# Attention values as weights in four column tiles, with the exponentials moving

## The chip, the cores and the metric

The kernel runs on one core of a Trainium2 chip. The metric is the device time in microseconds (us) of one execution. Before the change it is 306.41 us, the median of 3 runs (304.89 to 308.06). The engines are TensorE (PE, with its weight loads shown apart as PEld), VectorE (DVE), ScalarE (ACT), GpSimd (POOL) and SyncE (SP), which issues the DMAs.

## The reference

One sequence of 2048 tokens with 512 features is normalised and sent through two branches, whose results are added to the input.

```python
xn = layernorm(x)
# branch A: sliding-window attention, H = 32 heads of Dh = 16, window W = 256
q, k, v = split(xn @ wqkv)
scores = einsum('bhqd,bhkd->bhqk', q, k) * Dh ** -0.5
mask = (i - j >= 0) & (i - j < W)
p = softmax(where(mask, scores, -1e9))
A = einsum('bhqk,bhkd->bhqd', p, v) @ wo
# branch B: gated MLP with a mix over tokens
z = gelu(xn @ w_in)                       # 2048 x 1376
z1, z2 = z[:, :688], layernorm(z[:, 688:])
g = w_sp @ z2 + b_sp                      # 2048 x 2048 times 2048 x 688
B = (z1 * g) @ w_out
out = x + A + B
```

## The kernel before, in words

The tokens are cut into 16 blocks of 128. The program has two stages.

The first stage (up to about 61 us) normalises the blocks, transposes them into `xnT`, computes all of `z` (`do_z`, L419) with the GELU on ScalarE, normalises `z2`, and computes the first projections (the list `early`: keys and queries of the first four blocks, and the values of `VRING - 1` blocks). The reciprocal standard deviations come from a power on GpSimd (`rpow`, L254). GpSimd's queue begins with constants, a memset of the ones in `v_ring` (L378) and of the padding of `u_sb` (L380).

The second stage runs eight kinds of units in an order that the class `Plan` works out before the program is built. `Plan` holds estimated times for the units and lists them one after the other. Each engine then executes its own instructions strictly in that order. The units are:

- `quad`: scores of one key block against up to three query blocks for four heads, as four matmuls of 32 rows side by side in the array (L587), into two PSUM tiles of `ps_s` (three buffers). ScalarE then takes the exponential of each tile into `E` (L595). `E` has keys on the partitions and queries along the row. A head pair shares 32 rows: `k_ring` exists twice, with odd and with even heads set to zero (`emask`).
- `mask`: GpSimd (L604) cuts the diagonal block and VectorE (L609) the far block.
- `unit_av`: the value product of one query block and half of the heads (16). For each head and each of up to three key blocks, a 128x128 block of `E` is loaded as weights and 17 columns of `v_ring` move: 16 values and a column of ones, whose product is the row sum (L624). The result `o_t` has queries on the partitions. VectorE takes the reciprocal of the 16 row sums (L636) and multiplies (L637) into `o_norm`. After the second half, a DMA transpose on SP's queue (L645) makes `oT`, with features on the partitions.
- `unit_q`, `unit_k`, `unit_v`: further projections (L294, L271, L309), copied out of PSUM by VectorE (L304, L284, L318) into rings.
- `unit_g`: one of 16 matmuls of the mix over tokens (L513). After the last, VectorE forms the gated product `u_sb` (L520), and a DMA transposes it into `uT` (L527).
- `unit_out`: part 0 multiplies `oT` with `wo` (L552), part 1 adds `uT` with `w_out` (L558). VectorE adds the residual `x_ch` (L562), and SP stores the block (L563) and loads the next residual.

Three facts set the order of the work around the change. `unit_av`, the projections and `unit_out` all write into the pool `ps_y`, which has a single buffer: the next of them can start on TensorE only when VectorE has read the last one. `unit_g` has a bank of its own (`ps_g`), and its matmuls, with the score matmuls, are placed between the users of `ps_y`. And `E` has `EBUFS` buffers, which a value product frees; a `quad` that needs one waits for it. The last three outputs come after the planned order, in `ps_s`.

Of the kernel before, what the change touches and what calls it, by code (L numbers as in the profile page):

```python
# [8 lines left out]
P = 128  # L9
BF = mybir.dt.bfloat16  # L10
F32 = mybir.dt.float32
ACT = mybir.ActivationFunctionType
ALU = mybir.AluOpType

S_TOK = 2048
D = 512
H = 32
DH = 16
# [4 lines left out]
NDC = D // P  # L23
# [4 lines left out]
NFC = UPAD // P  # L28
Z_RANGES = [(0, 512), (512, FH)]
QRING = 8  # L30
VRING = 5
EBUFS = 12
X_DMA = 8


# [4 lines left out]
class Plan:  # L40


    PROJ = 0.86
    AV_PAIR = 0.0255
    OUT_MM = 0.215
    GCH = 0.144
    LAT = 0.36
# [13 lines left out]
    def run(self, proj, n_out_inline):  # L61
# [8 lines left out]
        o_at, u_at = {}, {}  # L70
# [3 lines left out]
        pend = []  # L74
# [4 lines left out]
        while qi < len(quads) or ai < len(avs) or oi < len(outs) or gi < len(gs) or proj:  # L79
            for rec in list(pend):  # L80
                if rec[0] <= self.tp + 0.2:
                    pend.remove(rec)
                    kb, G = rec[1]
# [7 lines left out]
            cand = []  # L91
            tq = 1e9
            if qi < len(quads):
                kb, G, e = quads[qi]
                ok = True
                if e == 0:
                    i = 4 * kb + G - EBUFS
                    if i >= 0:
                        k2, g2 = divmod(i, 4)
# [8 lines left out]
                if ok:  # L108
                    a, b = (2 * qi) % 3, (2 * qi + 1) % 3
# [3 lines left out]
            if ai < len(avs):  # L113
                qb, h = avs[ai]
                keys = [(kb, G) for kb in range(max(0, qb - 2), qb + 1) for G in (2 * h, 2 * h + 1)]
                if all(k in masked for k in keys) and not any(
# [3 lines left out]
                    n = sum(1 for k in keys) * 8  # L120
# [8 lines left out]
            if oi < len(outs):  # L129
                n, part = outs[oi]  # L130
# [5 lines left out]
            if gi < len(gs):  # L136
                n, hf, c = gs[gi]
                cand.append((self.gfree if c == 0 else 0.0, 5, "g", self.GCH))
            now = [x for x in cand if x[0] <= self.tp + 0.05]
            if not now:  # L140
                m = min(x[0] for x in cand)
# [9 lines left out]
            if pick[2] == "quad":  # L151
                kb, G, e = quads[qi]
                w = nblk(kb)
                order.append(("quad", kb, G, e))
                a, b = (2 * qi) % 3, (2 * qi + 1) % 3
                dur = {3: 0.755, 2: 0.55, 1: 0.34}[w]
                lat = self.LAT - 0.05 * (3 - w)
                for s in (a, b):
                    self.ta = max(self.ta, self.tp + lat) + dur
                    self.sfree[s] = self.ta + self.BACK  # L160
                self.tp += 0.14 + 0.054 * w
                if e == 1:
                    pend.append((self.ta + 0.05, (kb, G)))
                qi += 1
            elif pick[2] == "av":
                qb, h = avs[ai]
                order.append(("av", qb, h))
                self.tp += pick[3]
                self.yfree = self.evac(0.72)
                if h == 1:  # L170
                    o_at[qb] = self.yfree + 2.3
                av_emitted.add((qb, h))
                ai += 1
            elif pick[2] == "proj":
                p = pick[4]
                proj.remove(p)
                order.append(("proj", p[2], p[3]))
                self.tp += pick[3]
                self.yfree = self.evac({"k": 1.2, "q": 0.7, "v": 0.7}[p[2]])
                done_proj[(p[2],) + p[3]] = self.yfree  # L180
            elif pick[2] == "out":
                n, part = outs[oi]
                order.append(("out", n, part))
                self.tp += pick[3]
                if part == 1:
                    self.yfree = self.evac(0.7)
                oi += 1
            else:
                n, hf, c = gs[gi]
                order.append(("g", n, hf, c))  # L190
                self.tp += self.GCH
                if c == NB - 1:
                    self.gfree = self.evac(0.52)
                    if hf == 1:
                        u_at[n] = self.gfree + 2.3
                gi += 1
# [6 lines left out]
def kernel(  # L203
# [12 lines left out]
    nc = tc.nc  # L216
# [11 lines left out]
    z2_all = pers.tile([P, NB, FH], BF, name="z2_all")  # L228
    q_ring = pers.tile([P, NG, QRING * P], BF, name="q_ring")
    k_ring = pers.tile([P, NG, 2, QRING * P], BF, name="k_ring")  # L230
    v_ring = pers.tile([P, VRING, H, DH + 1], BF, name="v_ring")
    fmask = pers.tile([P, P], BF, name="fmask")
    emask = pers.tile([P, 2], F32, name="emask")
    esel = pers.tile([P, 4], F32, name="esel")
    b_bf = pers.tile([P, NB], BF, name="b_bf")
    b_all = pers.tile([P, NB], F32, name="b_all")
    mvx = pers.tile([P, NB, 2], F32, name="mvx")
# [68 lines left out]
    def unit_v(n, on_act=False):  # L306
        m = ps_y.tile([P, 512], F32, name="m", tag="y")
        for c in range(NDC):
            nc.tensor.matmul(  # L309
                m[:], lhsT=xnT[:, c, n * P : (n + 1) * P], rhs=wqkv[:, c, 2 * D : 3 * D],  # L310
                start=(c == 0), stop=(c == NDC - 1),
            )
        dst = v_ring[:, n % VRING, :, 0:DH]
        src = m[:].rearrange("p (h d) -> p h d", d=DH)
        if on_act:
            nc.scalar.copy(out=dst, in_=src)
        else:
            nc.vector.tensor_copy(out=dst, in_=src)  # L318
# [4 lines left out]
    with tc.tile_pool(name="win_pool", bufs=1) as winp, tc.tile_pool(  # L323
# [51 lines left out]
            out=esel[:], in_=esel[:], pattern=[[32, 4]], compare_op=ALU.is_ge,  # L375
            fill=0.0, base=DH - 1, channel_multiplier=-1,
        )
        nc.gpsimd.memset(v_ring[:, :, :, DH : DH + 1], 1.0)  # L378
        for u_sb in u_sbs:
            nc.gpsimd.memset(u_sb[:, FH:UPAD], 0.0)  # L380

# [66 lines left out]
        for n in range(NB + 3):  # L448
            if n < NB:
                transpose_x(n)  # L450
            if n + 3 < NB:
                norm_apply(n + 3)
            if n in stats_at:
                lo, hi = stats_at[n][0], stats_at[n][-1] + 1
                for i in range(lo, hi):
                    x_stats(i)
                rs_x(lo, hi)
            if n == 2:
                nc.vector.tensor_reduce(
                    out=emask[:, 0:1], in_=esel[:], op=ALU.add, axis=mybir.AxisListType.X  # L460
                )
                nc.vector.tensor_scalar(
                    out=emask[:, 1:2], in0=emask[:, 0:1], scalar1=-1.0, scalar2=1.0,
                    op0=ALU.mult, op1=ALU.add,
                )
                nc.vector.tensor_copy(out=b_all[:], in_=b_bf[:])
            if 2 <= n < NB + 2:
                do_z(n - 2, 1)
            if n >= 6 and early:
                f, a = early.pop(0)  # L470
                f(*a, on_act=True)
            if n >= 3:
                do_z(n - 3, 0)
                z2_stats(n - 3)
                if n % 2 == 0:
                    rs_z(n - 4, n - 2)
                elif n >= 5:
                    z2_norm(n - 5)
                    z2_norm(n - 4)
# [4 lines left out]
            f(*a, on_act=True)  # L484

    ep = ctx.enter_context(tc.tile_pool(name="ep", bufs=EBUFS))
    onp = ctx.enter_context(tc.tile_pool(name="onp", bufs=2))
    otp = ctx.enter_context(tc.tile_pool(name="otp", bufs=3))
    utp = ctx.enter_context(tc.tile_pool(name="utp", bufs=2))
    cpool = ctx.enter_context(tc.tile_pool(name="cpool", bufs=2))  # L490
    wsp_pool = ctx.enter_context(tc.tile_pool(name="wsp_pool", bufs=2))
# [48 lines left out]
    def unit_out(n, part, tail=False):  # L540
        if part == 0:
            load_xres(n)
            if tail:
                t = ps_s.tile([P, 2, 512], F32, name="mt", tag="S")
                fo_tiles[n] = t[:, 0, :]
            else:
                t = ps_y.tile([P, 512], F32, name="fo", tag="y")
                fo_tiles[n] = t[:]
            fo = fo_tiles[n]
            oT = oT_tiles.pop(n)  # L550
            for c in range(NDC):
                nc.tensor.matmul(fo, lhsT=oT[:, c, :], rhs=wo_sb[:, c, :], start=(c == 0), stop=False)  # L552
            return
        fo = fo_tiles.pop(n)
        uT = uT_tiles.pop(n)
# [55 lines left out]
                in1=fmask[:].unsqueeze(1).to_broadcast([P, 8, P]), op=ALU.mult,  # L611
            )

    o_state = {}

    def unit_av(qb, half):
        o_t = ps_y.tile([P, 16, DH + 1], F32, name="o_t", tag="y")
        kbs = [kb for kb in (qb - 2, qb - 1, qb) if kb >= 0]
        for g2 in range(2):
            G = 2 * half + g2  # L620
            for j in range(8):
                h = 8 * G + j
                for i, kb in enumerate(kbs):
                    nc.tensor.matmul(  # L624
                        o_t[:, 8 * g2 + j, :],
                        lhsT=E_tiles[(kb, G)][:, qb - kb, j, :],
                        rhs=v_ring[:, kb % VRING, h, :],
                        start=(i == 0),
                        stop=(i == len(kbs) - 1),
                    )  # L630
            E_tiles.pop((qb - 2, G), None)
        if half == 0:
            o_state["n"] = onp.tile([P, D], BF, name="o_norm")
        o_n = o_state["n"]
        rsum = sml.tile([P, 16], F32, name="rsum")
        nc.vector.reciprocal(out=rsum[:], in_=o_t[:, :, DH])  # L636
        nc.vector.tensor_tensor(  # L637
            out=o_n[:, half * 256 : (half + 1) * 256].rearrange("p (h d) -> p h d", d=DH),
            in0=o_t[:, :, 0:DH],
            in1=rsum[:].unsqueeze(2).to_broadcast([P, 16, DH]),  # L640
            op=ALU.mult,
        )
        if half == 1:
            oT = otp.tile([P, NDC, P], BF, name="oT")
            nc.sync.dma_start_transpose(out=oT[:], in_=o_n[:])  # L645
            oT_tiles[qb] = oT

    load_wsp(0)
    load_wsp(1)
# [60 lines left out]
```

## Time and profile before

| what | value |
|---|---|
| median of 3 runs | 306.41 us |
| profiled execution | 304.67 us |
| its span, from first to last instruction | 302.9 us |
| mean granted TensorE clock | 0.996 |
| last value product (L624) begins its last weight load | 284.7 us |
| value products, matmuls | 1440, of 171 ns each, overlapping |
| reciprocal of row sums (L636) | 32 of 258 ns |
| normalising multiply (L637) | 32 of 425 ns |

Busy time is the sum of an engine's instruction times. Matmuls overlap in a pipeline, so TensorE's busy time is no measure of how near it is to its peak. In a group's line, the figures after the bar are the busy time in us, the mean of one in ns, and the idle time just before them with what ended it. The chain that ended last is followed back from the last instruction, and its shares say which engine the end waited for.

### The profile page before, as it was taken

To read this page: it belongs to the slowest core of one execution; us is meant where nothing else is said; L and a number is where in the kernel's file an instruction comes from. 1 tells how busy PE (TensorE), PEld (TensorE's weight loads), DVE (VectorE), ACT (ScalarE), POOL (GpSimd) and SP (SyncE) were. 2 spreads that over 40 slices of the span, in tenths; PEclk is the share of its full clock that TensorE was granted. 3 is DMA by queue.
4 is the path that set the end of the run, shared out by engine and by line. 5 is a ranking of instruction groups with operands and counts; after the bars stand their busy time and mean duration, and the time that the engine had idled before them with its cause. 6 is when DMAs were issued, how large, how long until landed. Compare 5 with 4: busy or idle time off the path is not lost.

```text
span 302.9 us, 7530 instructions
## 1 busy us (share of the span) xinstructions
PE 281.2 (93%) x3168; PEld 153.8 (51%) x3168; DVE 168.0 (55%) x343; ACT 219.4 (72%) x315; POOL 91.1 (30%) x100
## 2 busy tenths in 40 slices
PE   1799999989998999899999999999998999999991
PEld 0465555534443556365555555555554555565640
DVE  4689995547755436355565654565486465342311
ACT  3378766699998798788788888768866788877100
POOL 6213420123433243222333322232222133444200
PEclk9999999999999999999999999999999999999998
DMA  7991237000416151714242624151514163425421
GB/s 231 306 299 36 46 60 156 0 3 0 103 38 123 38 113 38 108 43 102 66 97 56 87 56 105 44 98 48 112 37 91 41 107 80 95 54 97 63 60 55
DMA packets 68849, 25.67 MB, mean 85 GB/s; under 512 B 59936, under 2 KB 68304, under 8 KB 68816
## 3 DMA queue, kind: packets, MB, share of 16 engines
q1 hardware_dynamic: 68768, 25.19, 37.4%
q8 instruction: 25, 0.41, 0.6%
q14 instruction: 8, 0.07, 0.1%
q0 software_dynamic: 48, 0.00, 0.1%
HBM read 8.41 MB, written 2.10 MB: 35 GB/s over the span
## 4 chain that ended last, share of the span: by engine, by line
PE 83%; DMA 5%; DVE 4%; issue 3%; ACT 2%; SPq 1%; POOL 0%; DVEq 0%; POOLq 0%; ACTq 0%
PE gf L513 26%; PE o_t L624 12%; PE S L587 10%; PE zs L419 10%; PE fo L558 6%; PE m L271 5%; PE m L294 4%; PE fo L552 4%; PE m L309 4%; DMA xs<-in_A_x_dram 2%; DMA x_ch<-in_A_x_dram 2%; DMA uT<-u_sb 1%; DMA oT<-o_norm 1%; DVE E L609 1%; PE tp L408 1%
## 5 line engine op out<-in xcount | busy, mean ns | idle before, releaser
L595 ACT ACTIVATE E<-S 128x768 bf16<-128x768 f32 (+2 forms) x256 | 179.4, 772 | 39.2 <-issue 23.8
L604 POOL TENSOR_SCALAR_AFFINE_SELECT E<-E 128x1024 bf16<-128x1024 bf16 x64 | 73.6, 1150 | 148.6 <-ACT E L595 145.8
L513 PE MATMUL gf<-z_all,wspT 128*128 128x344 bf16 x512 | 92.8, 311 | 0.9 <-DVE u_sb L520 0.7
L513 PEld LDWEIGHTS <-wspT 128*128 128x128 bf16 x512 | 43.3, 97 | 32.9 <-issue 12.8
L609 DVE TENSOR_TENSOR E<-E,fmask 128x1024 bf16<-128x1024 bf16 x56 | 46.2, 825 | 2.3 <-ACT E L595 1.9
L587 PE MATMUL S<-q_ring,k_ring 32*128 32x384 bf16 (+2 forms) x576 | 44.6, 303 | 2.2 <-ACT E L595 2.1
L624 PEld LDWEIGHTS <-E 128*128 128x128 bf16 x1440 | 40.0, 96 | 4.3 <-issue 2.4
L419 PE MATMUL zs<-w_in_sb,xnT 128*128 128x512 bf16 (+1 forms) x256 | 41.8, 317 | 0.0
L624 PE MATMUL o_t<-v_ring,E 128*128 128x17 bf16 x1440 | 41.3, 171 | 0.2 <-DVE q_ring L304 0.2
L427 ACT ACTIVATE z_all<-zs 128x688 bf16<-128x688 f32 x32 | 23.8, 743 | 14.0 <-PE zs L419 14.0
L587 PEld LDWEIGHTS <-k_ring 32*128 32x128 bf16 x576 | 14.2, 91 | 35.9 <-issue 35.1
L419 PEld LDWEIGHTS <-xnT 128*128 128x128 bf16 x256 | 23.1, 100 | 16.5 <-issue 1.3
L636 DVE RECIPROCAL rsum<-o_t 128x16 f32<-128x16 f32 x32 | 8.2, 258 | 35.8 <-PE o_t L624 35.8
L562 DVE TENSOR_TENSOR out_sb<-fo,x_ch 128x512 bf16<-128x512 f32 x13 | 9.0, 692 | 31.0 <-PE fo L558 31.0
L520 DVE SCALAR_TENSOR_TENSOR u_sb<-gf,b_all,z_all 128x344 bf16<-128x344 f32 x32 | 18.3, 572 | 13.6 <-PE gf L513 13.6
L558 PE MATMUL fo<-w_out_sb,uT 128*128 128x512 bf16 x78 | 20.4, 382 | 0.8 <-DMA uT<-u_sb 0.8
L284 DVE TENSOR_TENSOR k_ring<-m,emask 128x1024 bf16<-128x1024 f32 x12 | 14.7, 1223 | 8.4 <-PE m L271 8.4
L259 DVE BATCH_NORM_STATS2 st<-z_all 128x6 f32<-128x344 bf16 x32 | 14.9, 506 | 6.3 <-ACT z_all L427 6.3
L309 PE MATMUL m<-wqkv,xnT 128*128 128x512 bf16 x64 | 16.5, 380 | 1.0 <-DVE k_ring L284 0.9
L294 PE MATMUL m<-xnT,wqkv 128*128 128x512 bf16 x64 | 16.5, 380 | 0.1
L558 PEld LDWEIGHTS <-uT 128*128 128x128 bf16 x96 | 8.3, 97 | 16.2 <-issue 8.5
L271 PE MATMUL m<-xnT,wqkv 128*128 128x512 bf16 x64 | 16.5, 380 | 0.0
(47 smaller groups left out, 152.5 us busy)
## 6 DMA issues: line engine op xcount, KB each, us to landing
x_ch<-in_A_x_dram SPq DMA_DIRECT2D x16, 128.0 KB, 2.2
out_dram<-out_sb SPq DMA_DIRECT2D x16, 128.0 KB, 1.7
xs<-in_A_x_dram SPq DMA_DIRECT2D x7, 256.0 KB, 10.6
wqkv<-in_A_wqkv_dram SPq DMA_DIRECT2D x1, 1536.0 KB, 11.6
w_in_sb<-in_B_w_in_dram SPq DMA_DIRECT2D x2, 688.0 KB, 6.2
w_out_sb<-in_B_w_out_dram SPq DMA_DIRECT2D x1, 640.0 KB, 9.5
wo_sb<-in_A_wo_dram SPq DMA_DIRECT2D x1, 512.0 KB, 10.5
xs<-in_A_x_dram SPq DMA_DIRECT2D x2, 128.0 KB, 2.1
```

Source lines behind the costliest of these rows:

```text
L271: nc.tensor.matmul(m[:], lhsT=wqkv[:, c, D + G * P : D + (G + 1) * P], rhs=xnT[:, c, grp * 512 : (grp + 1) * 512], start=(c == 0), stop=(c ...
L294: nc.tensor.matmul(m[:], lhsT=wqkv[:, c, G * P : (G + 1) * P], rhs=xnT[:, c, grp * 512 : (grp + 1) * 512], start=(c == 0), stop=(c == NDC ...
L309: nc.tensor.matmul(m[:], lhsT=xnT[:, c, n * P : (n + 1) * P], rhs=wqkv[:, c, 2 * D : 3 * D], start=(c == 0), stop=(c == NDC - 1),)
L419: nc.tensor.matmul(zp[:, lo:hi], lhsT=xnT[:, c, n * P : (n + 1) * P], rhs=w_in_sb[:, c, f0 + lo : f0 + hi], start=(c == 0), stop=(c == NDC ...
L427: nc.scalar.activation(out=dst[:, n, :], in_=zp[:, 0:FH], func=ACT.Gelu_apprx_tanh)
L513: nc.tensor.matmul(gf[:, 0:FQ], lhsT=w[:, c, :], rhs=z2_all[:, c, lo : lo + FQ], start=(c == 0), stop=(c == NB - 1),)
L558: nc.tensor.matmul(fo, lhsT=uT[0:kk, c, :], rhs=w_out_sb[0:kk, c, :], start=False, stop=(c == NFC - 1))
L587: nc.tensor.matmul(S[:, i, d0 : d0 + w], lhsT=k_ring[32 * s : 32 * s + 32, G, e, k0 : k0 + P], rhs=q_ring[32 * s : 32 * s + 32, G, s0 : s0 ...
L595: nc.scalar.activation(out=E[:, 0:nb, j : j + 3 : 2, :].rearrange("p b h c -> p h b c"), in_=tiles[pr][:, :, 0:ncol].rearrange("p h (b c) ...
L604: nc.gpsimd.affine_select(out=E[:, 0, :, :], in_=E[:, 0, :, :], pattern=[[0, 8], [1, P]], compare_op=ALU.is_ge, fill=0.0, base=0, channel_ ...
L609: nc.vector.tensor_tensor(out=E[:, 2, :, :], in0=E[:, 2, :, :], in1=fmask[:].unsqueeze(1).to_broadcast([P, 8, P]), op=ALU.mult,)
L624: nc.tensor.matmul(o_t[:, 8 * g2 + j, :], lhsT=E_tiles[(kb, G)][:, qb - kb, j, :], rhs=v_ring[:, kb % VRING, h, :], start=(i == 0), stop=( ...
```

## The change

The operands of the value product change places. The values of a head pair become the weights, 32 columns of 128 rows, and 128 columns of exponentials move. Four such matmuls, for four head pairs, write to the four 32-partition strips of one PSUM tile, each in its own column tile of the array. The even heads (`e = 0`) use the columns values, ones; the odd heads use ones, values: `v_ring` holds for each head pair four groups of 16 columns, of which the first and the last are values and the two in the middle are ones. The result has features on the partitions already, and each row sum stands 16 times, in the 16 partitions beside its head's values.

VectorE shuffles the tile by 16 partitions within each group of 32, so that row sums lie over values, takes the reciprocal of all of it, multiplies, and with a predicated copy puts the odd heads' rows over the even ones. The result is `oT`; the DMA transpose of `o_norm` is gone. `bmask` is a new constant that marks the odd heads' partitions.

`VRING` goes from 5 to 4, so one projection of values moves from the first stage to the second; `EBUFS` goes from 12 to 11. The planner's estimates for the value product change, and with them the order of the units in the second stage. `v_ring` is filled with ones as a whole.

```diff
-VRING = 5
-EBUFS = 12
+VRING = 4
+EBUFS = 11
...
-    AV_PAIR = 0.0255
+    AV_PAIR = 0.022
...
+            if not cand:
+                self.tp = min(rec[0] for rec in pend)
+                continue
...
-                self.yfree = self.evac(0.72)
+                self.yfree = self.evac(2.1) + 0.2
                 if h == 1:
-                    o_at[qb] = self.yfree + 2.3
+                    o_at[qb] = self.yfree + 0.3
...
-    v_ring = pers.tile([P, VRING, H, DH + 1], BF, name="v_ring")
+    v_ring = pers.tile([P, VRING, H // 2, 4, DH], BF, name="v_ring")
...
+    bmask = pers.tile([P, 2, P], mybir.dt.uint8, name="bmask")
...
-        dst = v_ring[:, n % VRING, :, 0:DH]
-        src = m[:].rearrange("p (h d) -> p h d", d=DH)
+        dst = v_ring[:, n % VRING, :, 0:4:3, :]
+        src = m[:].rearrange("p (h e d) -> p h e d", e=2, d=DH)
...
-        nc.gpsimd.memset(v_ring[:, :, :, DH : DH + 1], 1.0)
+        nc.gpsimd.memset(v_ring[:], 1.0)
...
+                nc.vector.tensor_copy(
+                    out=bmask[:], in_=emask[:, 1:2].unsqueeze(2).to_broadcast([P, 2, P])
+                )
...
-    onp = ctx.enter_context(tc.tile_pool(name="onp", bufs=2))
-    otp = ctx.enter_context(tc.tile_pool(name="otp", bufs=3))
+    onp = ctx.enter_context(tc.tile_pool(name="onp", bufs=1))
+    otp = ctx.enter_context(tc.tile_pool(name="otp", bufs=6))
...
-            oT = oT_tiles.pop(n)
             for c in range(NDC):
-                nc.tensor.matmul(fo, lhsT=oT[:, c, :], rhs=wo_sb[:, c, :], start=(c == 0), stop=False)
+                oT = oT_tiles[(n, c // 2)]
+                nc.tensor.matmul(
+                    fo, lhsT=oT[:, c % 2, 0, :], rhs=wo_sb[:, c, :], start=(c == 0), stop=False
+                )
...
     def unit_av(qb, half):
-        o_t = ps_y.tile([P, 16, DH + 1], F32, name="o_t", tag="y")
+        T = ps_y.tile([P, 2, 2, P], F32, name="o_t", tag="y")
         kbs = [kb for kb in (qb - 2, qb - 1, qb) if kb >= 0]
         for g2 in range(2):
             G = 2 * half + g2
-            for j in range(8):
-                h = 8 * G + j
+            for e in range(2):
                 for i, kb in enumerate(kbs):
-                    nc.tensor.matmul(
-                        o_t[:, 8 * g2 + j, :],
-                        lhsT=E_tiles[(kb, G)][:, qb - kb, j, :],
-                        rhs=v_ring[:, kb % VRING, h, :],
-                        start=(i == 0),
-                        stop=(i == len(kbs) - 1),
-                    )
+                    for s in range(4):
+                        hp = 4 * G + s
+                        nc.tensor.matmul(
+                            T[32 * s : 32 * s + 32, g2, e, :],
+                            lhsT=v_ring[:, kb % VRING, hp, 2 * e : 2 * e + 2, :].rearrange("p a d -> p (a d)"),
+                            rhs=E_tiles[(kb, G)][:, qb - kb, 2 * s + e, :],
+                            start=(i == 0),
+                            stop=(i == len(kbs) - 1),
+                        )
...
-        rsum = sml.tile([P, 16], F32, name="rsum")
-        nc.vector.reciprocal(out=rsum[:], in_=o_t[:, :, DH])
-        nc.vector.tensor_tensor(
-            out=o_n[:, half * 256 : (half + 1) * 256].rearrange("p (h d) -> p h d", d=DH),
-            in0=o_t[:, :, 0:DH],
-            in1=rsum[:].unsqueeze(2).to_broadcast([P, 16, DH]),
-            op=ALU.mult,
-        )
-        if half == 1:
-            oT = otp.tile([P, NDC, P], BF, name="oT")
-            nc.sync.dma_start_transpose(out=oT[:], in_=o_n[:])
-            oT_tiles[qb] = oT
+        R = onp.tile([P, 2, 2, P], F32, name="o_r")
+        nc.vector.stream_shuffle(out=R[:], in_=T[:], mask=[(i + DH) % 32 for i in range(32)])
+        nc.vector.reciprocal(out=R[:], in_=R[:])
+        oT = otp.tile([P, 2, 2, P], BF, name="oT")
+        nc.vector.tensor_tensor(out=oT[:], in0=T[:], in1=R[:], op=ALU.mult)
+        nc.vector.copy_predicated(out=oT[:, :, 0, :], mask=bmask[:], data=oT[:, :, 1, :])
+        oT_tiles[(qb, half)] = oT
```

More of the change, by code (lines that the diff above doesn't have):

```diff
@@ L612, in mask @@
             )
-    o_state = {}
     def unit_av(qb, half):
-        o_t = ps_y.tile([P, 16, DH + 1], F32, name="o_t", tag="y")
+        T = ps_y.tile([P, 2, 2, P], F32, name="o_t", tag="y")
         kbs = [kb for kb in (qb - 2, qb - 1, qb) if kb >= 0]
@@ L620, in unit_av @@
             G = 2 * half + g2
-            for j in range(8):
-                h = 8 * G + j
+            for e in range(2):
                 for i, kb in enumerate(kbs):
-                    nc.tensor.matmul(
-                        o_t[:, 8 * g2 + j, :],
-                        lhsT=E_tiles[(kb, G)][:, qb - kb, j, :],
-                        rhs=v_ring[:, kb % VRING, h, :],
-                        start=(i == 0),
-                        stop=(i == len(kbs) - 1),
-                    )
-            E_tiles.pop((qb - 2, G), None)
-        if half == 0:
-            o_state["n"] = onp.tile([P, D], BF, name="o_norm")
-        o_n = o_state["n"]
-        rsum = sml.tile([P, 16], F32, name="rsum")
-        nc.vector.reciprocal(out=rsum[:], in_=o_t[:, :, DH])
-        nc.vector.tensor_tensor(
-            out=o_n[:, half * 256 : (half + 1) * 256].rearrange("p (h d) -> p h d", d=DH),
-            in0=o_t[:, :, 0:DH],
-            in1=rsum[:].unsqueeze(2).to_broadcast([P, 16, DH]),
-            op=ALU.mult,
-        )
-        if half == 1:
-            oT = otp.tile([P, NDC, P], BF, name="oT")
-            nc.sync.dma_start_transpose(out=oT[:], in_=o_n[:])
-            oT_tiles[qb] = oT
+                    for s in range(4):
[7 more added lines that the diff above has]
+                        )
+            E_tiles.pop((qb - 2, G), None)
+        R = onp.tile([P, 2, 2, P], F32, name="o_r")
[5 more added lines that the diff above has]
+        oT_tiles[(qb, half)] = oT
     load_wsp(0)
```

## The prediction

> **What bounds it now.** I read the busy shares by engine first, then the chain that ended last, then the windows by stage, and then single units in the timeline.
>
> ```profile
> PE 281.2 (93%) x3168; PEld 153.8 (51%) x3168; DVE 168.0 (55%) x343; ACT 219.4 (72%) x315; POOL 91.1 (30%) x100
> PEclk9999999999999999999999999999999999999998
> PE 83%; DMA 5%; DVE 4%; issue 3%; ACT 2%; SPq 1%; POOL 0%; DVEq 0%; POOLq 0%; ACTq 0%
> ```
>
> TensorE ends last nearly everywhere, at full clock, so what the change saves there would count. The windows (us from the start; busy of PE, PEld, DVE, ACT, POOL) show the main stage:
>
> ```profile
> 72.00:285.00 213.00, 208.81 (x2711) 114.71 (x2708) 113.93 (x191) 171.09 (x245) 70.87 (x62) 1.00 0.37 75
> ```
>
> VectorE has half of this stage free. But share is not what matters: every value unit, projection and output shares one PSUM bank (`ps_y`, one buffer), and TensorE is refused the next of them until VectorE has read the last. The groups give the prices:
>
> ```profile
> L624 PE MATMUL o_t<-v_ring,E 128*128 128x17 bf16 x1440 | 41.3, 171 | 0.2 <-DVE q_ring L304 0.2
> L636 DVE RECIPROCAL rsum<-o_t 128x16 f32<-128x16 f32 x32 | 8.2, 258 | 35.8 <-PE o_t L624 35.8
> L562 DVE TENSOR_TENSOR out_sb<-fo,x_ch 128x512 bf16<-128x512 f32 x13 | 9.0, 692 | 31.0 <-PE fo L558 31.0
> L637 DVE TENSOR_TENSOR o_norm<-o_t,rsum 128x256 bf16<-128x256 f32 x32 | 13.6, 425 | 1.1
> ```
>
> and the timeline one hand-over of the bank (start, length, engine, line):
>
> ```profile
> 212.87 1.36 PE L624 MATMUL o_t<-v_ring,E 128*128 128x17 bf16 x48
> ...
> 214.17 0.34 PE L587 MATMUL S<-q_ring,k_ring 32*128 32x384 bf16 x4
> 214.27 0.26 DVE L636 RECIPROCAL rsum<-o_t 128x16 f32<-128x16 f32 x1 [0.62 <-PE o_t L624]
> ...
> 214.44 0.76 PE L513 MATMUL gf<-z_all,wspT 128*128 128x344 bf16 x4
> 214.56 0.42 DVE L637 TENSOR_TENSOR o_norm<-o_t,rsum 128x256 bf16<-128x256 f32 x1
> ```
>
> The bank is held 0.26 + 0.03 + 0.42 us by VectorE, plus about 0.04 and 0.10 for the two hand-overs: 0.85 us, covered by score and gate matmuls (L587, L513). That cover is what the change puts to the test.
>
> **The new VectorE chain.** Two instructions on 16 and 256 elements become a shuffle (512 fp32 from PSUM), a reciprocal (512, SBUF to SBUF), a multiply (512, PSUM with SBUF) and a predicated copy (256). The multiply has L562 as its row: 0.69 us. The shuffle is not in this trace; like the cast of 512 from PSUM (L304, 690 ns) I take 0.69, and between 0.41 (L394, 512 elements in SBUF) and 1.22 (L284, 1024) it moves the unit by -0.3 to +0.5. The predicated copy comes after the bank's last reader; at 0.42 (L637's size) it lies beside the next unit's matmuls.
>
> The reciprocal decides. VectorE instructions from PSUM cost 425 ns at 256 and 692 at 512: 1.04 ns an element over a fixed 158. The old reciprocal at 16 elements takes 258, so 100 ns over the fixed part, 6.25 ns an element. If that holds, 512 elements cost 158 + 512 x 6.25 = 3.36 us. If the 100 ns were fixed latency, it is 0.69 to 0.79; if SBUF sources also went at L394's rate, 0.41; if the fixed part were as small as 125, 8.3 ns an element and 4.4 us. I take 3.36, since 16 times one rate fits the row without a second constant.
>
> The Trainium skill speaks against this change here: "VectorE: DVE Perf Modes", section "First, the fixed hardware budget", says the reciprocal iterates a divide with a repeat count of 8. Eight cycles at the page's 0.96 GHz would make 512 elements about 4.4 us and the total some 34 us more than my sum; the trace row fits six better.
>
> So the bank is held 0.69 + 3.36 + 0.69 + 0.06 (gaps) + 0.14 (hand-overs) = 4.94 us.
>
> **TensorE's part.** Still 1440 matmuls. On the chain of waits 48 of the old pairs took 1.20 us, 25 ns each. The new ones move 128 columns in four column tiles. The nearest thing that runs tiles side by side is L587, four row tiles: by the chain 0.27 us for 384 columns and 0.17 for 128, hence 0.05 per 128 columns and 0.12 fixed. For a group of four that bounds 0.05 to 0.17 us; I keep 0.10, the old 4 x 25 ns: 36 us over 360 groups, with 19 and 61 as ends.
>
> The Trainium skill, "TensorE: Matmul & The Clock Gate", section "Measured speedup vs the span model", has three column tiles at 2.38 times one. That efficiency would make a group about 0.07 us and the total some 12 us less; no run here shows it.
>
> **The sum along the bank.** I went through the order that the planner's code emits (its sequence alone) and added, for each user of the bank, its matmuls and then the longer of "VectorE until the bank is free" and "matmuls queued before the next user", with a gate matmul 0.155 (26.2% of the span over 512) and a set of four score matmuls 0.27. Value units: 32, filler 0 to 3.1 us, always below 4.94; 36.0 of matmuls and 31 x 4.94 = 153.1. Projections: 12 q, 12 k, 13 v (one moves here from the start), 0.95 each and then the longer of 0.83 (1.36 for k) and filler, which is two score sets with 6 gates, 1.47, or 7 gates, 1.08, 26.2 + 30.2 + 28.6 = 85.0. Outputs, 13: 0.9 and 1.5 of matmuls, then filler: 46.5. Total 320.6. The same walk on the old order, with 0.85 held, gives 213.7; the first user starts at 61.4 and waits 1.7 for the table load, so it ends at 276.8, where the trace has 284.85: 8 us of stalls that it does not see. With VectorE's long holds covering many of them I add 4.
>
> The start moves. One early projection less is -0.9 (0.86 on the chain). The memset of `v_ring` grows from 160 to 4096 elements on GpSimd, ahead of the row statistics' power (L254, first at 4.94 us). Memset rows: 128 columns 0.20, 16 columns 0.11, so 0.85 ns an element and 3.5 us; the strided 160 took 0.77, 4.2 ns an element, up to 17. The chain has slack till the third tile's norm at 9.34, so +1.8 to about +13; dense filling is nearest to the first row, +2.5. Thus the last value unit's matmuls end at 61.4 - 0.9 + 2.5 + 1.7 + 320.6 + 4 = 389.3.
>
> The tail: output 13's addition queues behind that unit's four VectorE instructions (5.2), then 0.7, a residual load of 3.8, 0.7 + 2.7, 0.7 and 2.6 to the end as in the trace: 16.5 (18.0 before). Span 405.8. The profiled execution is 304.67 against a span of 302.9, so 1.8 goes on top: **407.6**. The median of the three runs, 306.41, is 0.6% over that execution; I say 407.
>
> Behind a bank user that must wait stand score and gate matmuls, since TensorE keeps its order, and behind the scores the exponentials; ScalarE has 171 us of work in the 213 of the main stage, less again in a longer one, so it catches up.
>
> The 16 transpose DMAs of `o_norm` leave SP's queue; only two waits on them show (1.3 and 1.0 us), worth nothing beside a bank that is late. Masks (0.82), gates' results (0.57) and the predicated copy on VectorE come between holds, while TensorE does 1 to 2.4 us of matmuls: hidden, except for the 4 us. VectorE's total becomes 168 + 32 x 5.16 - 21.8 + 0.9 = 312 us, below the span; the bank is the bound, not the engine.
>
> **Rivals.**
> 1. Slow reciprocal and worse: eight cycles an element (hold 6.0: 442), or TensorE, idle for 3.4 us per value unit (4.94 less 1.56 of filler on average), loses its clock. The windows show 1.00 still in 297 to 300, where no matmul runs, and 0.57 in 300 to 303: about four idle us cost the clock, and the gaps here come near that. Half clock on a third of the bank's 102 us of matmuls would add 34: 441. Chance 0.18.
> 2. The reciprocal from SBUF runs at double rate (1.8 us; hold 3.34): chain 271.0, total about 356. L263 and L394 (688 and 512 bf16 in 0.43 and 0.41) show double rates and more for SBUF sources; nothing does for a reciprocal. 0.06.
> 3. One element a clock (hold 2.27): chain 243.8, tail 13.8, total 328. For it: the 100 ns may be latency. Against: the exact fit. 0.10.
> 4. Not slower: the four column tiles stream abreast, L632 of the changed kernel at 0.053 a group, 19 us instead of 36. It decides only when the bank is held no more than about 2.0 us, so with the reciprocal at L394's 0.41: chain 221.1, total 305, level with before, and under it without the 4 us of stalls. Were the tiles not to overlap at all, groups cost 0.21 and 40 us are lost instead. 0.04.
>
> My forecast, 390 to 425, has 0.62. Range: that, most of rival 1, and down to rival 2: 352 to 450. About 1% is what a measurement here can tell from no change; faster 0.02, same 0.02, slower 0.96.
>
> **What would show it.** The reciprocal's mean near 3.4 us; bank users waiting mainly for the multiply; value groups near 0.10 us; TensorE's share falling to about 55 to 65%; the first normalised tile 2 to 3 us later; clock still near 1.00. It is wrong if the reciprocal costs about 0.7, if the clock drops, or if the column tiles do not overlap.

## The result and the profile after

The changed kernel takes 440.02 us (median of 4 runs, 436.91 to 444.43) against 305.87 us (median of 4). The ratio, 1.434 with a 95% interval of 1.418 to 1.450, leaves out the slowest run, 444.43 us at a mean clock of 0.831, beside 442.58 at 0.834 and 436.91 and 437.47 at 0.855. That slowest run is the profiled one. Its span is 442.7 us, it lies 1% above the median, and the terms below are summed against it.

From the page of the changed kernel: busy time by engine, the clock in 40 slices of the span, and the chain that ended last by engine and by line.

```profile
PE 327.4 (74%) x3168; PEld 150.9 (34%) x3168; DVE 310.5 (70%) x441; ACT 218.6 (49%) x314; POOL 91.2 (21%) x100
PEclk9999999688888766787989667876989889885568
PE 54%; DVE 39%; issue 3%; POOL 1%; ACT 1%; DMA 0%; SPq 0%; ACTq 0%; DVEq 0%
DVE o_r L642 24%; PE gf L520 13%; PE zs L423 9%; DVE o_r L641 5%; DVE oT L644 5%; PE m L275 5%; PE o_t L632 5%; PE m L298 4%; PE fo L567 4%; PE S L596 4%; PE fo L559 4%; PE m L313 4%; DVE E L618 3%; PE mt L567 1%; DVE u_sb L527 1%
```

VectorE was 4% of the chain and is now 39%, and one line, the reciprocal L642, is 24% of it. VectorE is busy for only 70% of the span: it is no saturated engine, it is what TensorE waits for. And the clock that TensorE is granted, full nearly throughout before, is now between 0.5 and 1.0 from the main stage on.

The groups of the value unit, in the same columns as before the change:

```profile
L642 DVE RECIPROCAL o_r<-o_r 128x512 f32<-128x512 f32 x32 | 107.3, 3353 | 1.1
L632 PE MATMUL o_t<-E,v_ring 128*32 128x128 bf16 x1440 | 29.6, 238 | 15.2 <-DVE oT L644 12.7
L641 DVE STREAM_SHUFFLE o_r<-o_t 128x512 f32<-128x512 f32 x32 | 23.2, 725 | 0.0
L644 DVE TENSOR_TENSOR oT<-o_t,o_r 128x512 bf16<-128x512 f32 x32 | 22.1, 691 | 1.1
```

One unit in the timeline (start, length, engine, line; the bracket is the idle time before):

```profile
217.49 0.85 PE L632 MATMUL o_t<-E,v_ring 128*32 128x128 bf16 x48
...
218.41 0.73 DVE L641 STREAM_SHUFFLE o_r<-o_t 128x512 f32<-128x512 f32 x1
...
219.17 3.35 DVE L642 RECIPROCAL o_r<-o_r 128x512 f32<-128x512 f32 x1
...
222.56 0.69 DVE L644 TENSOR_TENSOR oT<-o_t,o_r 128x512 bf16<-128x512 f32 x1
223.28 0.43 DVE L645 COPY_PREDICATED oT<-bmask,oT 128x256 bf16<-128x256 uint8 x1
223.30 1.02 PE L275 MATMUL m<-xnT,wqkv 128*128 128x512 bf16 x4 [3.38 <-DVE oT L644]
```

The chain of waits has the value matmuls end at 218.37. The next user of the bank starts at 223.30, as soon as the multiply has ended: the bank was held for 4.93 us. TensorE's score and gate matmuls in between were done by 219.9, and then it stood idle for 3.38 us. The 48 value matmuls themselves take 0.81 us on the chain, where the old ones took 1.20.

### The profile page after: what moved, and what is told of

Same layout as the page of the kernel before. It is cut to its first block, busy times and chain, and to the rows that moved or that the text cites. A ratio compares the mean times of both kernels' runs of the same rounds, so it can differ in the third digit from the quotient of the medians.

```text
span 442.7 us, 7580 instructions
## 1 busy us (share of the span) xinstructions
PE 327.4 (74%) x3168; PEld 150.9 (34%) x3168; DVE 310.5 (70%) x441; ACT 218.6 (49%) x314; POOL 91.2 (21%) x100
## 4 chain that ended last, share of the span: by engine, by line
PE 54%; DVE 39%; issue 3%; POOL 1%; ACT 1%; DMA 0%; SPq 0%; ACTq 0%; DVEq 0%
DVE o_r L642 24%; PE gf L520 13%; PE zs L423 9%; DVE o_r L641 5%; DVE oT L644 5%; PE m L275 5%; PE o_t L632 5%; PE m L298 4%; PE fo L567 4%; PE S L596 4%; PE fo L559 4%; PE m L313 4%; DVE E L618 3%; PE mt L567 1%; DVE u_sb L527 1%
## 5 line engine op out<-in xcount | busy, mean ns | idle before, releaser
L520 PE MATMUL gf<-z_all,wspT 128*128 128x344 bf16 x512 | 109.5, 356 | 3.3 <-DVE u_sb L527 3.2
L642 DVE RECIPROCAL o_r<-o_r 128x512 f32<-128x512 f32 x32 | 107.3, 3353 | 1.1
L596 PE MATMUL S<-q_ring,k_ring 32*128 32x384 bf16 (+2 forms) x576 | 59.0, 353 | 7.8 <-ACT E L604 5.9
L632 PE MATMUL o_t<-E,v_ring 128*32 128x128 bf16 x1440 | 29.6, 238 | 15.2 <-DVE oT L644 12.7
L275 PE MATMUL m<-xnT,wqkv 128*128 128x512 bf16 x64 | 22.0, 481 | 23.0 <-DVE oT L644 23.0
L632 PEld LDWEIGHTS <-v_ring 128*32 128x32 bf16 x1440 | 24.2, 105 | 23.6 <-issue 23.0
L298 PE MATMUL m<-xnT,wqkv 128*128 128x512 bf16 x64 | 20.8, 458 | 13.6 <-DVE oT L644 13.6
L641 DVE STREAM_SHUFFLE o_r<-o_t 128x512 f32<-128x512 f32 x32 | 23.2, 725 | 0.0
L559 PE MATMUL fo<-wo_sb,oT 128*128 128x512 bf16 x52 | 17.9, 477 | 7.1 <-DVE oT L644 7.1
L644 DVE TENSOR_TENSOR oT<-o_t,o_r 128x512 bf16<-128x512 f32 x32 | 22.1, 691 | 1.1
L308 DVE CAST q_ring<-m 128x512 bf16<-128x512 f32 x12 | 8.3, 691 | 17.3 <-PE m L298 17.3
## 6 DMA issues: line engine op xcount, KB each, us to landing
wqkv<-in_A_wqkv_dram SPq DMA_DIRECT2D x1, 1536.0 KB, 11.5
wo_sb<-in_A_wo_dram SPq DMA_DIRECT2D x1, 512.0 KB, 11.5
```

Of the source, the lines that this page charges most:

```text
L275: nc.tensor.matmul(m[:], lhsT=wqkv[:, c, D + G * P : D + (G + 1) * P], rhs=xnT[:, c, grp * 512 : (grp + 1) * 512], start=(c == 0), stop=(c ...
L520: nc.tensor.matmul(gf[:, 0:FQ], lhsT=w[:, c, :], rhs=z2_all[:, c, lo : lo + FQ], start=(c == 0), stop=(c == NB - 1),)
L596: nc.tensor.matmul(S[:, i, d0 : d0 + w], lhsT=k_ring[32 * s : 32 * s + 32, G, e, k0 : k0 + P], rhs=q_ring[32 * s : 32 * s + 32, G, s0 : s0 ...
L632: nc.tensor.matmul(T[32 * s : 32 * s + 32, g2, e, :], lhsT=v_ring[:, kb % VRING, hp, 2 * e : 2 * e + 2, :].rearrange("p a d -> p (a d)"), ...
L641: nc.vector.stream_shuffle(out=R[:], in_=T[:], mask=[(i + DH) % 32 for i in range(32)])
L642: nc.vector.reciprocal(out=R[:], in_=R[:])
```

## The experiments

**The reciprocal taken out.** The shuffled sums go straight into the multiply.

```diff
-        nc.vector.reciprocal(out=R[:], in_=R[:])
```

> The changed kernel without its reciprocal (L642): the multiply takes the shuffled row sums themselves, so the division of the softmax is left out. Theory (the one bank is held 4.97 us per value unit, 3.35 of it by the reciprocal): the hold falls to 1.59 us, the walk along the bank from 310 to 217 us, TensorE has no long gaps and keeps its clock (over 0.97), and the time comes to 300 to 312 us. Rival (the swapped operands, the smaller rings or the new order cost the time): the time stays over 380 us.

Measured: 323.7 us, 1.059 times before (1.055 to 1.063), mean clock 0.946. That is 116 us less than the changed kernel, so one instruction carries nearly all of the change, and the rival falls. The time is 12 us above the forecast's upper end, though, and the clock lower than it said. The windows of this run (us; busy of PE, PEld, DVE, ACT, POOL; granted clock; DMA) say where:

```profile
220.00:260.00 40.00, 38.74 (x474) 19.71 (x473) 29.88 (x46) 27.95 (x40) 12.01 (x10) 1.00 0.32 61
260.00:290.00 30.00, 23.73 (x312) 11.06 (x311) 14.83 (x28) 18.49 (x29) 8.72 (x7) 0.85 0.28 50
290.00:305.00 15.00, 12.08 (x198) 6.17 (x198) 6.63 (x14) 10.13 (x28) 6.70 (x6) 0.50 0.01 2
```

From 220 to 260 us TensorE is as full as before the change (38.7 of 40 us; before, 38.8). After that its work thins out, and from 290 us it runs at half clock.

**The same, planned for the hold that is left.** The planner put gate matmuls behind holds of 2.3 us that no longer exist, and had none left for the end.

```diff
-    AV_PAIR = 0.022
+    AV_PAIR = 0.0175
...
-                self.yfree = self.evac(2.1) + 0.2
+                self.yfree = self.evac(1.45)
...
-        nc.vector.reciprocal(out=R[:], in_=R[:])
```

> The run without the reciprocal (324 us) with the planner told the hold that then remains (1.45 instead of 2.1 + 0.2 us, and 0.0175 us per value matmul); the division is left out again. Theory (its last 45 us were slow because the gate matmuls, spent as filler for longer holds, had run out, and the clock fell to a half there): 303 to 314 us, with the clock over 0.97. Rival (shuffle, multiply and copy still hold the bank too long): 320 to 328 us.

Measured: 310.6 us, 1.014 times before (1.010 to 1.018), clock 0.985, as the theory had it: 13 us come from the order alone.

```profile
260.00:290.00 30.00, 27.32 (x455) 13.96 (x455) 17.00 (x32) 24.28 (x45) 14.31 (x12) 0.97 0.25 42
290.00:308.00 18.00, 10.15 (x97) 4.37 (x86) 5.76 (x11) 1.21 (x4) 1.91 (x2) 0.78 0.18 48
```

With gates left for the end, the window 260 to 290 is nearly full (27.3 of 30) and at clock 0.97. Even without any reciprocal, then, the swapped operands with shuffle, multiply and copy (each over 256 to 512 elements) gain nothing.

**Half of the reciprocal.**

```diff
-        nc.vector.reciprocal(out=R[:], in_=R[:])
+        nc.vector.reciprocal(out=R[:, 0], in_=R[:, 0])
```

> The changed kernel with the reciprocal on 256 of the 512 elements (half of the heads stay multiplied by their row sum's raw value, so the division is left out for them). The hold falls from 4.97 to 3.37 us. Theory (time follows the hold, 31 x 1.6 = 50 us, and TensorE's idle time per value unit falls under 2 us, so that the clock comes back in part): 350 to 380 us, clock 0.9 or more. Rival (the lost clock is the larger part and stays): 385 to 405 us.

Measured: 375.6 us, 1.227 (1.223 to 1.231), clock 0.933. The group's line gives the second point of the reciprocal's price:

```profile
L642 DVE RECIPROCAL o_r<-o_r 128x256 f32<-128x256 f32 x32 | 56.1, 1753 | 1.1
```

In one and the same order the reciprocal costs 0, 1.75 and 3.35 us, and the kernel takes 323.7, 375.6 and 440.0. The first half adds 52 us, where 31 holds x 1.75 make 54. The second adds 61 to 64 (to 436.91 and to 440.0), where 31 x 1.60 make 50. So the first half is paid at its length, and the second at its length and some 11 to 14 us more, while the clock falls from 0.93 to between 0.83 and 0.86.

**The old kernel with a reciprocal in its hold.** The operands, rings and order before the change; only VectorE's work between the row sums and the multiply grows.

```diff
         nc.vector.reciprocal(out=rsum[:], in_=o_t[:, :, DH])
+        for _ in range(3):
+            nc.vector.reciprocal(out=junk[:], in_=junk[:])
```

> The kernel before, with three reciprocals of 160 constant elements put between the reciprocal and the multiply of each value unit: about 3 x 1.16 us = 3.5 us more in the hold of the bank, and nothing else changed. Theory (the hold alone explains the change): the walk along the old order gives about 397 us at full clock, and the clock falls, so 395 to 430 us. Rival (the hold is hidden in the old order, and the new operand order is what costs): under 340 us.

Measured: 427.9 us, 1.400 (1.396 to 1.403), clock 0.856. Nothing of the swap is needed to bring about the loss: 3.47 us in the hold of this bank and the clock that goes with it suffice. (The three reciprocals average 1134 ns, 3.40 us for all.)

```profile
164.92 3.47 DVE L640 RECIPROCAL junk<-junk 128x160 f32<-128x160 f32 x3
168.31 0.36 DVE L641 TENSOR_TENSOR o_norm<-o_t,rsum 128x256 bf16<-128x256 f32 x1
...
168.73 1.89 PE L310 MATMUL m<-wqkv,xnT 128*128 128x512 bf16 x4 [3.35 <-DVE o_norm L641]
```

The timeline shows the same picture in the old code: a projection waits 3.35 us for the multiply, and its four matmuls then take 1.89 us.

**TensorE kept busy during the wait.** The first two sets of score matmuls after each value unit are repeated.

```diff
-            for i in range(2):
+            for i in [0, 1] * (5 if warm[0] > 0 else 1):
```

> The changed kernel, with the score matmuls of the first two sets after each value unit repeated five times (same values written again), so that TensorE works through part of the wait for the bank. The repeats add about 1 us per set of TensorE work, inside the 4.97 us hold. Theory (the excess over the forecast of 407 us is the lost clock): the granted clock rises from 0.83 to 0.95 or more and the time falls to 405 to 418 us, though more is computed. Rival (the excess is VectorE's other work between the holds): the clock rises too, but the time stays at 432 to 448 us.

Measured: 425.8 us, 1.394 (1.390 to 1.398), clock 0.928. More work, and 11 to 14 us less time. It lies between the two theories: the clock came back for a part only, and the time with it. A second run:

> A second look at the changed kernel with repeated score matmuls (426 us), for the clock of the projections that follow a wait. Theory: as in the first, waits of TensorE are mostly 2.1 us or less, and 3 or 4 in 5 of the projections after them run at full clock (about 1.0 us and not 1.87); 423 to 429 us. Rival: the share differs from run to run, and the time with it, by more than 1%.

Measured: 426.9 us (a single run), clock 0.915. The time repeats within 0.3%. Waits for the multiply are mostly 2.1 us here, but of the 14 projections that waited 1.9 to 2.4 us only 7 took about 1.0 us, fewer than expected; the others took 1.35 to 1.87.

**The planner told the true hold.**

```diff
-                self.yfree = self.evac(2.1) + 0.2
+                self.yfree = self.evac(4.4) + 0.2
...
-                    yq.append((max(self.yfree, o_at[n], u_at[n] - 0.8), 3, "out", 4 * self.OUT_MM))
+                    yq.append((max(self.yfree, o_at[n], u_at[n] - 0.8), 1.5, "out", 4 * self.OUT_MM))
```

> The changed kernel with the planner's estimate of VectorE's work on a value unit at 4.4 instead of 2.1 us (and outputs preferred over value units, since the order has no solution without it), so that more matmuls lie behind the value units and fewer behind the projections. Theory (the bank's hold sets the pace, whatever the order): 425 to 440 us. Rival (the order, planned for a hold of half the length, is what costs the time): under 400 us.

Measured: 430.2 us, 1.407 (1.403 to 1.411), clock 0.86. Planning for 2.3 us instead of 4.9 had cost some 10 us, not the 130 that were lost.

**A version with 16 reciprocals again.** The swapped value product stays. VectorE turns the tile back in blocks of 32x32, so that queries are on the partitions and one reciprocal per head and query is enough; only the first turn holds the bank.

```diff
-        R = onp.tile([P, 2, 2, P], F32, name="o_r")
-        nc.vector.stream_shuffle(out=R[:], in_=T[:], mask=[(i + DH) % 32 for i in range(32)])
-        nc.vector.reciprocal(out=R[:], in_=R[:])
...
+        nc.vector.transpose(out=R[:].rearrange("p e k c -> p (e k c)"), in_=T[:].rearrange("p e g q -> p (e g q)"))
+        nc.vector.reciprocal(out=rsum[:], in_=R[:, :, :, DH])
+        nc.vector.tensor_tensor(
+            out=o_n[:].rearrange("p k e d -> p e k d"), in0=R[:, :, :, 0:DH],
+            in1=rsum[:].unsqueeze(3).to_broadcast([P, 2, 8, DH]), op=ALU.mult,
+        )
+        nc.vector.transpose(out=oT[:].rearrange("p g q -> p (g q)"), in_=o_n[:].rearrange("p k e d -> p (k e d)"))
```

> A version that keeps the swapped operands but takes the reciprocal away from the bank: VectorE turns the tile in 32x32 blocks out of PSUM (512 elements), takes 16 reciprocals as before the change, multiplies 256 elements in SBUF and turns the 256 results back; both heads of a pair use the columns values, ones; the planner is told 0.76 us for the bank and 1.15 us after it; the memset of ones is spread behind the first tiles. Theory: the bank is held about 0.87 us again, the walk along it gives 208 us instead of 310, TensorE keeps its clock, and the cheaper value matmuls (0.81 instead of 1.2 us per unit) are worth 12 us: 292 to 302 us, under the kernel before. Rival (1.1 us more of VectorE per unit, though off the bank, delays the next evacuation as much as it saves): 303 to 318 us.

Measured: 307.2 us, 1.004 (1.001 to 1.006), clock 0.998. All of the loss is gone, and nothing is gained. Its groups:

```profile
L639 DVE STREAM_TRANSPOSE o_r<-o_t 128x512 f32<-128x512 f32 x32 | 22.9, 715 | 19.1 <-PE o_t L630 18.8
L641 DVE RECIPROCAL rsum<-o_r 128x16 f32<-128x16 f32 x32 | 8.1, 253 | 1.1
```

From 62 to 285 us TensorE has 206.4 us of work here (the sum of its windows) against 217.4 before, as the cheaper value matmuls promise; but the last value unit ends about 7 us later than before. VectorE has 155 us of work in that stretch instead of 119, and what was saved on TensorE went into waiting. The time lies within the rival's range. Whether VectorE's order is the reason was asked by one more run, in which the three instructions after the first turn are put behind the evacuation of the bank's next user:

```diff
+            flush()
             unit_av(*op[1:])
         elif op[0] == "proj":
             units[op[1]](*op[2])
+            flush()
```

> The version with the turned tile (307 us), with its three instructions that don't need the bank (16 reciprocals, multiply, turning back, 1.1 us) put behind the evacuation of the bank's next user instead of ahead of it. Theory (VectorE's order delayed those evacuations; TensorE had 11 us less work in the main stage than before the change, but stood idle 18 us more): 296 to 304 us. Rival (VectorE only trades one delay for another, since the same 1.1 us now stand ahead of the masks): 305 to 310 us.

Measured: 324.5 us, 1.060 (1.055 to 1.064): slower than both answers. In the waits GpSimd's masks now stand for 12.1 us (3 times, up to 5.2) until VectorE's turning back has ended, and ScalarE's exponentials for 19.3 us until the masks have (11.5 in the run before). Which of VectorE's instructions must come first so that the 11 us are gained stays open; no version here beats the kernel before.

## Why the prediction was right

The direction, the bound and the price of the reciprocal were right, and 440 lies in the range of 352 to 450. But it lies above the 390 to 425 that the forecast claimed, and it is in the range only because that took in most of rival 1, the lost clock, at a chance of 0.18. The forecast had the clock near 1.00 and named a falling clock as a sign of being wrong; the clock fell, and most of the 33 us above 407 are put down to it below.

- **The reciprocal.** Forecast 3.36 us from one row with 16 elements; measured 3.353. The points 16 (253 ns, from SBUF), 256 (1753) and 512 (3353) lie on one line, 153 ns and 6.25 ns an element. (160 elements average 1134, 2% under the line.) It is a price per element, not a latency, and rivals 2 and 3 fall: reading SBUF brings no double rate (at 16 elements 253 ns, against 258 from PSUM). That the reciprocal's fixed part is that of the multiply, 153 against 158, was luck; the row alone allowed 125, and with it 4.4 us. The eight cycles that I had worked out from the Trainium skill's "VectorE: DVE Perf Modes", section "First, the fixed hardware budget", would be 8.3 ns; the measurement decides for six cycles of its 0.96 GHz.
- **The hold.** Shuffle 0.725 for 0.69, multiply 0.691 for 0.69, together with the hand-overs 4.93 for 4.94.
- **The value matmuls.** 0.81 us for 48, so 0.068 per group of four column tiles, where I kept the old 0.10: 1440 x (25.0 - 16.9) ns = 11.7 us less than forecast. The estimate from the Trainium skill's "TensorE: Matmul & The Clock Gate", section "Measured speedup vs the span model" (2.38 for three column tiles), was about 0.07 and 12 us; this run agrees with it. Rival 4 asked for 0.053, and for a short hold, and got neither.
- **The start.** The memset of `v_ring` took 3.51 us, as worked out, and the first matmul of `z` starts 1.9 us later than before (12.11 against 10.20) where I had 2.5. **The tail** took 15.4 us from the last value matmul (427.3) to the end, for 16.5.
- **VectorE's other work.** I added 4 us for everything that the walk doesn't see. The far masks alone stand for 12.6 us on the chain of 62 to 443 us (3.3% of it): the step that called masks and gates' results hidden between the holds was too kind by some 9 us. That the cheaper value matmuls nearly make up for it is luck.
- **The clock, the term that was mis-placed.** The forecast had it "near 1.00", and rival 1 had "half clock on a third of the bank's matmuls, 441". Terms so far: 407.6 - 11.7 - 0.6 - 1.1 + 8.6 = 402.8, so about 42 us are left (34 if 436.91 is taken for the time), from the clock and what else I don't see. An estimate from the other side: eight TensorE lines make up 47.4% of the chain of those 381 us, 181 us, and the mean of the clocks that the windows from 62 to 425 show is 0.80; at full clock a fifth less, 36 us. Piece by piece, 104 us of the TensorE work on the chain lie in stretches at half clock, so 52 us is the most that the full clock could take off it.

How the clock is lost shows in two waits of the changed kernel's timeline. First one of 1.7 us, then one of 3.4:

```profile
211.94 1.07 PE L559 MATMUL fo<-wo_sb,oT 128*128 128x512 bf16 x4 [1.75 <-DVE oT L644]
...
214.78 0.90 PE L520 MATMUL gf<-z_all,wspT 128*128 128x344 bf16 x5
```

```profile
171.45 1.87 PE L298 MATMUL m<-xnT,wqkv 128*128 128x512 bf16 x4 [3.40 <-DVE oT L644]
...
173.69 1.90 PE L520 MATMUL gf<-z_all,wspT 128*128 128x344 bf16 x6
```

The same four matmuls of 512 columns take 1.07 us after the short wait and 1.87 after the long one, and six gates 1.90 where five take 0.90. Of the 18 projections before 400 us that waited 2.5 us or more for the multiply, 13 ran at 1.86 to 1.87 us from the start; the other 5 began at 1.02 to 1.04, and the six gates behind them took 1.83 to 1.90. The six projections and outputs that waited 1.8 us or less in that time ran at full clock.

The length of a wait is not the rule, though. With half of the reciprocal, 15 projections waited 1.78 to 1.81 us, and 5 of them ran at half clock nearly from the start. Two of these waits, both of 1.80 us, lie in these windows (from 218.88 to 220.68 and from 230.63 to 232.43; the figure after POOL is the granted clock):

```profile
217.59:221.00 3.41, 1.47 (x9) 0.62 (x10) 3.31 (x4) 2.92 (x4) 0.70 (x2) 1.00 0.15 31
221.00:224.42 3.42, 3.28 (x13) 0.99 (x11) 1.86 (x4) 1.51 (x2) 1.03 (x1) 0.50 0.00 0
227.83:231.25 3.42, 2.67 (x63) 1.37 (x61) 2.74 (x5) 1.81 (x3) 0.00 (x0) 1.00 0.28 81
231.25:234.66 3.41, 2.17 (x15) 0.92 (x16) 3.17 (x6) 1.95 (x4) 1.32 (x1) 1.00 0.02 5
```

The windows are cut where the clock can change. In every trace here the granted clock is either 1 or 0.5, and it changes only on a grid of 3.413 us that is fixed for the run; the changed kernel's 45 changes all lie on one. The first wait falls into one interval of the grid, which leaves TensorE 1.47 us of work in it, and the next interval runs at half clock; the second is split over two. In the changed kernel 22 of the 23 intervals before a drop had TensorE busy for at most 60% (the other for 73%), and the 58 that were followed by no drop for 58 to 100%. A wait of 3.4 us empties most of an interval or half of two; whether the clock falls during it or a microsecond later depends on the grid. No long wait is needed either: in the run without a reciprocal the clock fell at 287.58 after an interval with 1.87 us of work and no wait over 0.42 us. The end of the old trace, from which I took that about four idle us cost the clock, fits too: the last matmul ends at 296.33, and the clock falls at 300.42, when the first empty interval is over. The Trainium skill, "TensorE: Matmul & The Clock Gate", section "What's actually happening", has a free-running window of about 3.4 us after which an idle array goes to half rate; the grid agrees with it, but here a window that was about half empty was often enough.

That the clock is a cause and not a companion is shown in part: repeating score matmuls inside the waits raised it from between 0.83 and 0.86 to 0.93 and took 11 to 14 us off, with more work done. The full 36 us are an estimate, since no run restored the full clock with the full hold. The hold itself is shown from both sides: taken out of the new kernel (324 us) and put into the old one (428 us).

## What to carry to other kernels

Before an instruction is moved from 16 elements to 512, find its price per element, even from a small row: subtract the fixed part of a neighbour on the same engine. An engine at 55% can become the bound through one buffer that must be read before the next matmul; count the time that it holds that buffer, and compare it with the work placed behind it. And when waits leave TensorE idle for about half of a stretch of 3.4 us, again and again, add a term for its clock.

## What the runs showed of the hardware

- VectorE's reciprocal of fp32 costs 153 ns and 6.25 ns an element (253, 1753 and 3353 ns for 16, 256 and 512 elements), six times the 1.04 of an addition or a multiply that reads PSUM.
- Four column tiles of 32 columns run side by side: 48 matmuls of 128 moving columns in 0.81 us, 16.9 ns each, less than the 25 ns of the old pairs with a 128-column load and 17 moving columns. Four untiled matmuls of 512 columns take 1.02 us, about 64 ns for 128 columns.
- VectorE turns 512 fp32 elements in blocks of 32x32 out of PSUM in 0.715 us, and 256 bf16 elements in SBUF in 0.445.
- TensorE's granted clock is 1 or 0.5 and changes only on a grid of 3.413 us, in all 11 traces. In the changed kernel, intervals with TensorE busy for at most 60% came before 22 of 23 drops. Waits of 2.56 to 3.65 us for the multiply cost all 18 projections before 400 us the clock, at once or within 1.4 us; with half of the reciprocal, 5 of 15 waits of 1.8 us did, by where they lay on the grid.
